# Attention with a learned position bias and two gated layers: an early table request on ScalarE and another order for the first two attention units

## The chip, the cores and the metric

The kernel runs on one core of one Trainium2 chip. The metric is the device time of an execution in microseconds (us); of several executions the median is given.

## The reference

Three stages follow one another, all in fp32. Only the first is touched by the change.

```python
# B, H, S, D = 2, 8, 576, 64
scores = q @ k.T / sqrt(D)
x = log1p(|i - j|) / log1p(max(i, 1))            # per pair of positions
bias = relu(x * w1 + b1) @ w2                    # 32 hidden units -> 8 heads
attn = softmax(scores + bias)                    # sum + 1e-9
x = attn @ v                                     # (1152, 512)
x = (silu(x @ w_gate) * (x @ w_val)) @ w_out     # 1536 hidden
# then a top-1 routed layer: 8 experts, capacity 288, 1024 hidden, relu
```

## The kernel before

**The bias.** For every position i the bias is a row over j. The kernel makes it in 36 groups of 16 rows. A group is: four `tensor_scalar` maxima on VectorE (`bias_t4`, line 107, tile `bt`, eight buffers), a product with `w2` on TensorE (`bias_mm`, line 125: eight matmuls), two evacuations on ScalarE that scale, add the constant `ncst` and mirror the row (`bias_evac`, lines 143 and 150, tile `bo`, four buffers), and a store by SP's queue to DRAM (line 154). `load_bias` (lines 165 to 167) reads the rows back, skewed, as a tile `bias_sb` of one block of 128 positions and one pair of heads. `ncst` is computed once at the start from `b1` and `w2` (a product of one column, folded by VectorE at line 313).

**The lead.** Eleven groups (`LEAD`) are made ahead of the attention loop. Between them, SP's queue issues further loads of queries and keys: after the store of the first group a query load and a key load, after that of the eighth another key load and the first two `load_bias`. The first scores (`qk(0)`) are computed after the tenth group, and the maxima of the twelfth are made before the loop starts.

**The units.** A unit is one block of 128 positions, one pair of heads and one batch: 32 of these, and four at the end that hold the last 64 positions of both batches. Every engine works its own queue in order, and the order is written out by hand: in each pass u of the loop, the names of the list `ORDER` are gone through, and each name issues its instructions if there is work for it. For head j = 0 or 1 of the pair the names are:

- `S`: VectorE adds the bias to the scores and takes the row minimum (line 203, tile `e_sb`)
- `E`: ScalarE's exponential with its sum (line 211)
- `R`: VectorE's reciprocal of the sum (lines 220 and 221)
- `N`: GpSimd normalises `e_sb` in place (line 225)

For the unit before it:

- `T0`, `T1`, `T2`: TensorE transposes three of the nine 128-column blocks of both heads (line 237, tile `ps_t`, two buffers); `T1` takes the end of the first head and the beginning of the second
- `V0`, `V2`: ScalarE evacuates the first and the last of these (line 248); `V1`: VectorE the middle one (line 246)

For the unit before that, `AV` is the product with the values and `XH`, `XL` its evacuation. `Q` computes the scores of the next unit (line 186). For the bias groups, counted from 0: `B0` to `B3` are the four maxima of group u + 12, `M0` and `M1` the product of group u + 11 (in two parts if its row is longer than 512 columns; a single part is `M1`), `BE0` and `BE1` its evacuation, `BE1` one pass later. `J` is a job for a later stage, none of which exists before pass 29.

In pass 0 there is no earlier unit. What is left of `ORDER` is S0 S1 B0 E0 E1 R0 B1 R1 Q B2 N0 B3 N1 M1; in pass 1 it is T0 S0 T1 S1 V1 BE1 B0 E0 E1 R0 B1 R1 V0 T2 Q B2 N0 B3 V2 N1 M1.

**After attention** the two projections, the output projection and routing, and the experts follow.

Of the kernel before, what the change touches and what calls it, by code (L numbers as in the profile page):

```python
# [14 lines left out]
AF = mybir.ActivationFunctionType  # L15
# [7 lines left out]

ORDER = (
    "G0 T0 S0 T1 G1 S1 V1 J AV BE1 B0 E0 E1 R0 J B1 M0 R1 J BE0 XH V0 T2 "
    "Q B2 XL J N0 B3 V2 N1 M1"
).split()

TAIL = [
    "T0 S0 T1 S1 E0 E1 V0 V1 R0 R1 N0 N1 AV XH T2 G0 XL V2 J J J J".split(),
    "T0 V0 T1 V1 AV T2 V2 XH XL G1".split(),
# [2 lines left out]
LEAD = 11  # L36
# [5 lines left out]
def attention(tc, ident, shape, qd, kd, vd, wb, geo, xh, xl, late):  # L42
    nc = tc.nc
# [16 lines left out]
    with ExitStack() as ctx:  # L60
# [15 lines left out]
        nc.sync.dma_start(geo_sb[:, :cut], geo[:, :cut])  # L76
        nbp, dist_sb, nips = geo_sb[:, :NB], geo_sb[:, NB:NB + S], geo_sb[:, NB + S:]
        ncst = cst.tile([P, 1], F32, name="ncst")
        kst = cst.tile([P, B * NP, S], F32, name="kst")
        vn = cst.tile([P, NP, B, NT_, 2 * D], F32, name="vn")  # L80
        bias_d = dr.tile([(S + 1) * H * PITCH], F32, name="bias_d")
# [20 lines left out]
        def bias_t4(R, a=0, b=4):  # L102
            m = span(R)
            for t4 in range(a, b):
                r = R * 4 + t4
                t = wk.tile([P, S], F32, tag="bt", name="bt", bufs=8)
                nc.vector.tensor_scalar(t[:, :m], dist_sb[:, :m], nbp[:, r:r + 1], None, ALU.max)  # L107
                bt_t[R, t4] = t
# [3 lines left out]
        def cuts(R):  # L112
            m = span(R)
            return [(0, m)] if m <= 512 else [(0, m // 2), (m // 2, m)]

        def bias_mm(R, part, wide=None):
            if part >= len(cuts(R)):
                return
            m0, m1 = cuts(R)[part]
            if wide is None:  # L120
                ps = ps_m.tile([P, 512], F32, tag="m", name="ps_b")
            else:
                ps = wide[part]
            for t4 in range(4):
                nc.tensor.matmul(
                    ps[t4 * GW:(t4 + 1) * GW, :m1 - m0], wb2, bt_t[R, t4][:, m0:m1], start=True, stop=True
                )
            bp_t[R, part] = ps
# [45 lines left out]
        groups = [c * GPC + n for c in order for n in range(GPC) if c * GPC + n < NG]  # L174
        NU = len(units)
# [126 lines left out]
        with tc.manual_schedule():  # L302
            korder = [(b, p) for p in range(NP) for b in range(B)]
            load_k(*korder[0])
            nc.sync.dma_start(geo_sb[:, cut:], geo[:, cut:])
            qt0 = order[0] * B
            load_q(qt0)
            nc.vector.tensor_scalar(dist_sb[:, :GEO0], dist_sb[:, :GEO0], w1c, None, ALU.mult)
            nc.vector.tensor_scalar(nbp, nbp, b1c, -1.0, ALU.mult, ALU.mult)
            ps_c = ps_m.tile([P, 512], F32, tag="m", name="ps_c")  # L310
            for t4 in range(4):
                nc.tensor.matmul(ps_c[t4 * GW:(t4 + 1) * GW, 0:1], wb2, b1c, start=True, stop=True)
            nc.vector.tensor_scalar_mul(ncst, ps_c[:, 0:1], -1.0 / SCALE)

            for n in range(LEAD):
                R = groups[n]
                bias_t4(R)
                if n < GPC:
                    wide = ps_s.tile([P, 2, 512], F32, tag="S", name="ps_w")
                    wide = wide[:, 0], wide[:, 1]  # L320
                elif n == GPC + 1:
                    wide = [
                        pool.tile([P, 512], F32, tag=tag, name="ps_w2") for pool, tag in ((ps_m, "m"), (ps_v, "x"))
                    ]
                else:
                    wide = [ps_t.tile([P, 512], F32, tag="T", name="ps_w2") for _ in cuts(R)]
                for part in range(2):
                    bias_mm(R, part, wide)
                if n == 0:
                    nc.vector.reciprocal(nips, nips)  # L330
                    nc.vector.tensor_scalar(dist_sb[:, GEO0:], dist_sb[:, GEO0:], w1c, None, ALU.mult)
                for part in range(2):
                    bias_evac(R, part)
                if n == 0:
                    load_q(qt0 + 1)
                    load_k(*korder[1])
                if n == GPC - 1:
                    load_k(*korder[2])
                    load_bias(order[0], 0)
                    load_bias(order[0], 1)  # L340
                elif n == GPC + 1:
                    qk(0)
            bias_t4(groups[LEAD])
            for u in range(NU + 2):
                n = LEAD + u
                g = groups[n] if n < NG else None
                g1 = groups[n + 1] if n + 1 < NG else None
                gp = groups[n - 1] if LEAD <= n - 1 < NG else None
                qc = order[u // 8 + 1] * B if u // 8 < NF else None
                if u < NU:  # L350
                    c, p, b = units[u]
                    for x in range(3, NU):
                        if units[x][2] in (0, None) and u == max(x - 2, x // 8 * 8 - 1, 0):
                            load_bias(*units[x][:2])
                    if u + 3 < len(korder):
                        load_k(*korder[u + 3])
                    if u % 2 == 0 and u // 2 < NP:
                        load_v(u // 2)
                    if RAW0 <= u < RAW0 + 4:
                        early_raw(*divmod(u - RAW0, 2))  # L360
                    if u % 4 == 0 and qc is not None:
                        load_q(qc + u % 8 // 4)
                live, prev, old = u < NU, 1 <= u <= NU, u >= 2
                two = g is not None and len(cuts(g)) == 2
                steps = {
                    "T0": (prev, lambda: transposes(u - 1, 0)),
                    "T1": (prev, lambda: transposes(u - 1, 1)),
                    "T2": (prev, lambda: transposes(u - 1, 2)),
                    "V0": (prev, lambda: t_evac(u - 1, 0)),
                    "V1": (prev, lambda: t_evac(u - 1, 1)),  # L370
                    "V2": (prev, lambda: t_evac(u - 1, 2)),
                    "BE1": (gp is not None, lambda: bias_evac(gp, len(cuts(gp)) - 1)),
                    "S0": (live, lambda: softmax(u, 0)),
                    "S1": (live, lambda: softmax(u, 1)),
                    "E0": (live, lambda: exp(u, 0)),
                    "E1": (live, lambda: exp(u, 1)),
                    "R0": (live, lambda: recip(u, 0)),
                    "R1": (live, lambda: recip(u, 1)),
                    "N0": (live, lambda: normalise(u, 0)),
                    "N1": (live, lambda: normalise(u, 1)),  # L380
                    "B0": (g1 is not None, lambda: bias_t4(g1, 0, 1)),
                    "B1": (g1 is not None, lambda: bias_t4(g1, 1, 2)),
                    "B2": (g1 is not None, lambda: bias_t4(g1, 2, 3)),
                    "B3": (g1 is not None, lambda: bias_t4(g1, 3, 4)),
                    "M0": (two, lambda: bias_mm(g, 0)),
                    "BE0": (two, lambda: bias_evac(g, 0)),
                    "M1": (g is not None, lambda: bias_mm(g, len(cuts(g)) - 1)),
                    "AV": (old, lambda: av(u - 2)),
                    "Q": (u + 1 < NU, lambda: qk(u + 1)),
                    "XH": (old, lambda: evac(u - 2, 0)),  # L390
                    "XL": (old, lambda: evac(u - 2, 1)),
                }
                for name in ORDER if u < NU - 1 else TAIL[u - NU + 1]:
                    if name == "J":
                        if u >= JOB0 and spare:
                            spare.pop(0)()
                    elif name in ("G0", "G1"):
                        if u == NU - 1 + int(name[1]):
                            gate0(int(name[1]))
                    elif steps[name][0]:  # L400
                        steps[name][1]()
                if u == NU:
                    late["idle"]()
                if u == NU - 1:
                    nc.scalar.activation(ncst, ncst, AF.Sigmoid)
                if u == NU + 1:
                    late["act"]((psg[0], psg[1]), wk.tile([P, S], F32, tag="bt", name="sg0", bufs=8))
# [824 lines left out]
```

## Time and profile before

| | |
|---|---|
| three timed executions | 591.12, 591.99, 592.31 us |
| their median | 591.99 us |
| the profiled execution | 588.43 us |
| its span, first to last instruction | 586.6 us |
| TensorE busy in the span | 535.1 us (91%) |
| VectorE busy | 393.5 us (67%) |
| ScalarE busy | 267.0 us (46%) |
| GpSimd busy | 93.3 us (16%) |
| mean granted TensorE clock | 0.961 of 2.4 GHz |

Rows of the trace are from the profiled execution, and times in them are us from the start of its span. PE is TensorE, PEld its weight load, DVE is VectorE, ACT is ScalarE, POOL is GpSimd, SPq is SyncE's queue. Ends of matmuls are modelled.

### The profile page before, as it was taken

The numbers are of one execution on the slowest core, as the hardware profiler recorded it, in microseconds if no ns is written. First come the engines' busy times: TensorE is split into PE (matmuls) and PEld (weight loads), VectorE is DVE, ScalarE is ACT, GpSimd is POOL, SyncE is SP. The second block draws the span as 40 slices with busy tenths as digits, with TensorE's granted clock in tenths as the row PEclk, the third lists the DMA queues.
The fourth block names the chain that finished last, engine by engine and source line by source line (L and its number), as shares of the span: only waits on it lengthen the run. The fifth ranks groups of instructions, "written<-read, shape, count | busy, mean of one in ns | idle before, by whom it ended". The sixth has DMA issues, their size and how long they took to land. (4 is left out here: it accounts for less than half of the span.)

```text
span 586.6 us, 10919 instructions
## 1 busy us (share of the span) xinstructions
PE 535.1 (91%) x3864; PEld 424.7 (72%) x3864; DVE 393.5 (67%) x1033; ACT 267.0 (46%) x578; POOL 93.3 (16%) x156
## 2 busy tenths in 40 slices
PE   6799999999999999999999999999979488299894
PEld 2366666666778899989999899997766285187673
DVE  7799999997776599999988475344451352244631
ACT  5677787787666345555343043222221150243420
POOL 0133333333333000000000000000231101210402
PEclk9899999999999999999999999999989879589898
DMA  5897436635331999854312121006119626900101
GB/s 189 293 318 236 142 122 198 197 113 183 110 84 57 286 357 341 297 184 160 108 73 94 50 80 65 1 31 258 46 61 340 234 83 254 322 4 1 44 1 44
DMA packets 49811, 88.87 MB, mean 151 GB/s; under 512 B 7986, under 2 KB 27444, under 8 KB 49728
## 3 DMA queue, kind: packets, MB, share of 16 engines
q1 hardware_dynamic: 48032, 84.11, 42.9%
q0 software_dynamic: 1552, 3.70, 1.8%
q8 instruction: 44, 0.72, 0.5%
q14 instruction: 39, 0.32, 0.2%
q10 hardware_dynamic: 144, 0.02, 0.0%
HBM read 66.73 MB, written 22.28 MB: 152 GB/s over the span
## 5 line engine op out<-in xcount | busy, mean ns | idle before, releaser
L488 PE MATMUL ps_gv<-xh,hl 128*128 128x384 f32 x528 | 135.5, 337 | 1.4 <-ACT hl L471 0.8
L488 PEld LDWEIGHTS ps_gv<-xh,hl 128*128 128x128 f32 x528 | 95.3, 188 | 2.8 <-ACT hl L471 1.5
L488 PE MATMUL ps_gv<-xl,hl 128*128 128x384 f32 x264 | 88.7, 336 | 0.0
L225 POOL TENSOR_SCALAR e_sb<-e_sb,rs 128x576 f32<-128x576 f32 x72 | 58.4, 821 | 127.4 <-DVE rs L221 98.4
L735 PE MATMUL ps_o<-hl,hh 128*128 128x512 f32 x216 | 72.4, 403 | 0.0
L107 DVE TENSOR_SCALAR bt<-geo_sb 128x320 f32<-128x320 f32 (+17 forms) x144 | 69.3, 517 | 0.0
L211 ACT ACTIVATE e_sb<-e_sb,mn 128x576 f32<-128x576 f32 x72 | 55.1, 768 | 15.9 <-DVE mn L203 15.9
L203 DVE CUSTOM_DVE_ANT_0 e_sb<-ps_s,bias_sb 128x576 f32<-128x576 f32 x72 | 51.3, 748 | 13.1 <-PE ps_s L186 5.9
L237 PEld LDWEIGHTS ps_t<-ident,e_sb 128*128 128x128 f32 x324 | 34.6, 142 | 30.8 <-POOL e_sb L225 15.3
L237 PE MATMUL ps_t<-ident,e_sb 128*128 128x128 f32 x324 | 52.0, 288 | 1.5 <-DVE et L246 1.1
L186 PE MATMUL ps_s<-kst,qst 64*128 64x288 f32 x320 | 49.3, 426 | 3.4 <-DVE mn L203 3.4
L488 PEld LDWEIGHTS ps_gv<-xl,hl 128*128 128x128 f32 x264 | 49.6, 188 | 0.1
L735 PEld LDWEIGHTS ps_o<-hl,hh 128*128 128x128 f32 x216 | 40.6, 188 | 10.0 <-issue 1.4
L559 POOL DMA_INDIRECT disp<-y,rsi x9 | 9.0, 1000 | 225.0 <-DVE rs L683 209.8
L735 PE MATMUL ps_o<-hl,hlo 128*128 128x512 f32 x105 | 42.1, 401 | 0.0
L266 PE MATMUL ps_x<-et,vn 128*64 128x128 f32 (+1 forms) x640 | 40.5, 269 | 0.0
L186 PEld LDWEIGHTS ps_s<-kst,qst 64*128 64x128 f32 x320 | 28.2, 186 | 15.3 <-issue 5.2
L471 ACT CAST hl<-dg 128x512 fp32r<-128x512 f32 x34 | 20.4, 620 | 39.0 <-PE ps_o L735 21.6
L498 ACT CAST hh<-sg 128x384 fp32r<-128x384 f32 x36 | 18.4, 511 | 38.3 <-DVE sg L497 38.0
L266 PEld LDWEIGHTS ps_x<-et,vn 128*64 128x64 f32 x640 | 31.7, 136 | 4.4
L248 ACT COPY et<-ps_t 128x384 f32<-128x384 f32 x72 | 31.2, 483 | 1.0 <-PE ps_t L237 1.0
L1059 PE MATMUL ps_h<-dxh,hl 128*128 128x288 f32 x128 | 29.5, 324 | 0.8 <-ACT dxh L458 0.8
(204 smaller groups left out, 910.1 us busy)
## 6 DMA issues: line engine op xcount, KB each, us to landing
raw<-e SPq DMA_DIRECT2D x24, 512.0 KB, 7.8
bias_d<-bo SPq DMA_DIRECT2D x36, 295.5 KB, 2.3
eraw<-e SPq DMA_DIRECT2D x16, 512.0 KB, 7.8
raw<-wo SPq DMA_DIRECT2D x12, 512.0 KB, 5.0
raw<-wg SPq DMA_DIRECT2D x11, 512.0 KB, 4.7
raw<-wv SPq DMA_DIRECT2D x11, 512.0 KB, 6.0
disp<-zero SPq DMA_DIRECT2D x9, 520.0 KB, 7.9
bias_sb<-bias_d SPq DMA_DIRECT2D x16, 288.0 KB, 3.6
```

The costliest lines, as they stand in the source:

```text
L107: nc.vector.tensor_scalar(t[:, :m], dist_sb[:, :m], nbp[:, r:r + 1], None, ALU.max)
L186: nc.tensor.matmul(pss[j][:, half, :HS], qst[c * B + bb][d, p], kst[d, bb * NP + p, half * HS:(half + 1) * HS], start=bb == bbs[0], stop=b ...
L203: nc.vector.tensor_tensor_reduce(out=e[:, j, :].rearrange("p (a n) -> p a n", a=2), in0=ps[:, :, :HS], in1=bias_sb[c, p][:, j, :].rearrang ...
L211: nc.scalar.activation(e[:, j, :], e[:, j, :], AF.Exp, bias=mn[:, j:j + 1], scale=-1.0, accum_out=sm[:, j:j + 1])
L225: nc.gpsimd.tensor_scalar(e[:, j, :], e[:, j, :], rs, 1.0, ALU.mult, ALU.mult)
L237: nc.tensor.transpose(ps[:, n * P:(n + 1) * P], e[:, o:o + P], ident)
L248: nc.scalar.copy(dst, ps)
L266: nc.tensor.matmul(ps[j * D:(j + 1) * D, o:o + n], vn[:, p, bb, jc, j * D:(j + 1) * D], et[:, t0:t0 + n], start=False, stop=jc == NF - 1, ...
L471: lambda: nc.scalar.copy(dh, g),
L488: nc.tensor.matmul(ps[:, :TN], w_[:, n, kc, :], x_[:, kc, t * TN:(t + 1) * TN], start=i == 0, stop=i == 3 * KC - 1,)
L735: nc.tensor.matmul(ps, ht_cols(f, a, tg), wot[f][b_], start=i == 0, stop=i == len(ops) - 1)
L1059: nc.tensor.matmul(ps[:, :CAP], part(e, f // 2, a)[:, kc, f % 2 * P:(f % 2 + 1) * P], x_[:, kc], start=i == 0, stop=i == 3 * KC - 1,)
```

## The change

At the start, ScalarE gets an exponential of one column, of a zero that VectorE has written to `ncst`. It stands behind the issue of the load of `wb_sb`, which is on ScalarE's queue too. `ncst` gets its value afterwards, as before.

Pass 0 and pass 1 have lists of their own. In pass 0 both reciprocals and both normalisations stand ahead of the four maxima, the scores of the next unit stand last (on TensorE, where they are alone now), and the product `M1` is gone. In pass 1 this product, of group 11, stands behind `T1` under the name `MF`. The rest of pass 1 is as before, `BE1` ahead of `E0` and `E1` too.

```diff
+FIRST = (
+    "S0 S1 E0 E1 BE1 R0 R1 N0 N1 B0 B1 B2 B3 Q"
+).split()
+SECOND = [x for step in ORDER for x in ((step, "MF") if step == "T1" else (step,))]
...
         ncst = cst.tile([P, 1], F32, name="ncst")
+        nc.vector.memset(ncst, 0.0)
+        nc.scalar.activation(ncst, ncst, AF.Exp)
...
             bias_t4(groups[LEAD])
+            assert len(cuts(groups[LEAD])) == 1
...
                     "M1": (g is not None, lambda: bias_mm(g, len(cuts(g)) - 1)),
+                    "MF": (True, lambda: bias_mm(gp, 0)),
...
-                for name in ORDER if u < NU - 1 else TAIL[u - NU + 1]:
+                for name in FIRST if u == 0 else SECOND if u == 1 else ORDER if u < NU - 1 else TAIL[u - NU + 1]:
```

## Rows read from the trace of the kernel before

**Rows 1.** Windows, from attention unit 2 on: busy time by engine, granted clock, DMA
```profile
core 0: us, PE busy (x) PEld busy (x) DVE busy (x) ACT busy (x) POOL busy (x), PEclk, DMA share, GB/s
30.00:120.00 90.00, 90.00 (x866) 56.90 (x865) 86.90 (x262) 68.48 (x169) 32.84 (x40) 1.00 0.61 199
```

**Rows 2.** Timeline of ScalarE, lead: start, duration, instruction, idle time before it
```profile
6.12 1.28 ACT L143 ACT_TABLE_LOAD   x1 [6.12 <-DVE geo_sb L330]
7.42 0.62 ACT L143 ACTIVATE bo<-ps_w,ncst,geo_sb 128x320 f32<-128x320 f32 x1
...
8.65 0.60 ACT L143 ACTIVATE bo<-ps_w,ncst,geo_sb 128x304 f32<-128x304 f32 x1
...
13.80 0.55 ACT L143 ACTIVATE bo<-ps_w,ncst,geo_sb 128x240 f32<-128x240 f32 x1 [0.93 <-PE ps_w L125]
```

**Rows 3.** Timeline of TensorE, lead: the last matmuls of the first and second group
```profile
5.76 1.33 PE L125 MATMUL ps_w<-bt,wb_sb 128*32 128x320 f32 x4
...
7.32 1.29 PE L125 MATMUL ps_w<-bt,wb_sb 128*32 128x304 f32 x4
```

**Rows 4.** Timeline of SP's queue, lead
```profile
8.53 0.33 SPq L154 DMA_DIRECT2D bias_d<-bo  x1
...
9.38 0.46 SPq L85 DMA_DIRECT2D kst<-kd  x1
9.95 0.36 SPq L154 DMA_DIRECT2D bias_d<-bo  x1
```

**Rows 5.** The tile `bo` from 9.9 to 10.0 us: the second store, issue to landing
```profile
DMA to landing us min/median/max: 3.7/3.7/3.7
```

**Rows 6.** Timeline of VectorE, late lead to unit 2
```profile
13.66 1.44 DVE L107 TENSOR_SCALAR bt<-geo_sb 128x384 f32<-128x384 f32 x4
...
22.82 0.76 DVE L203 CUSTOM_DVE_ANT_0 e_sb<-ps_s,bias_sb 128x576 f32<-128x576 f32 x1 [2.49 <-DMA bias_sb<-bias_d]
...
25.58 0.15 DVE L220 TENSOR_SCALAR rs<-sm 128x1 f32<-128x1 f32 x1
...
25.85 1.37 DVE L107 TENSOR_SCALAR bt<-geo_sb 128x384 f32<-128x384 f32 x2
27.13 0.74 DVE L203 CUSTOM_DVE_ANT_0 e_sb<-ps_s,bias_sb 128x576 f32<-128x576 f32 x1
...
28.94 0.56 DVE L246 COPY et<-ps_t 128x384 f32<-128x384 f32 x1 [0.38 <-PE ps_t L237]
...
30.30 0.15 DVE L220 TENSOR_SCALAR rs<-sm 128x1 f32<-128x1 f32 x1
...
31.93 0.74 DVE L203 CUSTOM_DVE_ANT_0 e_sb<-ps_s,bias_sb 128x576 f32<-128x576 f32 x1
```

**Rows 7.** Timeline of TensorE, units 0 to 2
```profile
23.64 0.75 PE L186 MATMUL ps_s<-kst,qst 64*128 64x288 f32 x2 [3.06 <-DVE mn L203]
...
25.87 1.56 PE L125 MATMUL ps_b<-bt,wb_sb 128*32 128x400 f32 x8
27.36 1.54 PE L237 MATMUL ps_t<-ident,e_sb 128*128 128x128 f32 x6
29.55 0.55 PE L237 MATMUL ps_t<-ident,e_sb 128*128 128x128 f32 x3 [0.65 <-DVE et L246]
...
34.04 0.55 PE L237 MATMUL ps_t<-ident,e_sb 128*128 128x128 f32 x3
...
35.69 0.83 PE L125 MATMUL ps_b<-bt,wb_sb 128*32 128x368 f32 x8
```

**Rows 8.** Timeline of ScalarE, units 0 and 1
```profile
27.55 0.69 ACT L143 ACTIVATE bo<-ps_b,ncst,geo_sb 128x400 f32<-128x400 f32 x1 [2.00 <-issue]
...
28.53 0.77 ACT L211 ACTIVATE e_sb<-e_sb,mn 128x576 f32<-128x576 f32 x1
...
29.95 0.19 ACT L211 ACTIVATION_READ_ACCUMULATOR e_sb<-e_sb,mn 128x1 f32 x1
```

**Rows 9.** Timeline of GpSimd, unit 0
```profile
25.43 1.57 POOL L225 TENSOR_SCALAR e_sb<-e_sb,rs 128x576 f32<-128x576 f32 x2 [24.13 <-DVE rs L221]
```

**Rows 10.** Windows, unit 0 to 1 (columns as in rows 1)
```profile
25.80:29.20 3.40, 3.10 (x15) 1.34 (x14) 3.02 (x8) 1.65 (x4) 1.20 (x2) 0.50 1.05 328
```

## The prediction

> **What bounds the kernel now.** I read the busy time by stage first, then the queues of the first 35 us one engine at a time, because the change touches nothing later. The stage view [rows 1] shows TensorE busy for the whole of 30 to 120 us and VectorE for 86.9 of these 90: from attention unit 2 on, TensorE is the bound, with VectorE close behind. Time that is won or lost before about 34 us is therefore a shift of TensorE's start into that stretch, and it is carried to the end; the 586.6 us span lies in an execution of 588.43 us, 3.56 us below the median of the three timed runs (591.99), so I work out a difference on the profile and lay it on the median.
>
> In the lead (4 to 23 us) the first evacuation by ScalarE starts at 7.42 us, right behind a table load of 1.28 us [rows 2]. The reader should not take 1.28 us for the price. The first group's product ends at 5.76 + 1.33 = 7.09, so without the load the evacuation would wait until then; the second group's product ends at 7.32 + 1.29 = 8.61, and the second evacuation starts at 8.65, so that one was not held by the load at all [rows 2, 3].
>
> What can carry the first 0.33 us further is SP's queue. The first store of bias rows (8.53) stands ahead of a query load and a key load (9.38), and the second store (9.95) takes 3.7 us to land, because it travels behind them [rows 4, 5]. The sixth evacuation waits at 13.80 [rows 2] for that landing, as there are four `bo` buffers. From there copy, product, store and re-load lead to the first softmax, which waits at 22.82 for `bias_sb` [rows 6].
>
> In units 0 and 1 the order is: TensorE does the bias product M1 of unit 0 at 25.87, then the transposes T0 and T1 of unit 0 at 27.36, then idles until T2 at 29.55, which waits for the evacuation V1 [rows 7]. ScalarE evacuates M1 (BE1) at 27.55 and starts the first exponential of unit 1 at 28.53, as soon as BE1 lets it [rows 8].
>
> **The change part by part.**
>
> *The table load.* It moves to ScalarE's empty start. Its new writer and reader of `ncst` cost VectorE one memset and one wait before the fold of the constant; both lie before 4.5 us beside the first loads, when ScalarE has nothing else to do: nothing, at most some 0.1 us if the wait became an instruction of its own. The gain is 7.42 − 7.09 = 0.33 us for the first evacuation and the first store. The two loads and the second store move with it, and through the sixth evacuation the first softmax too. Bounds: 0 if the landing of the second store is not the last to come at 13.80, 0.33 by the products' ends, 1.28 if these ends are modelled far too late. I take **−0.3 us**.
>
> *FIRST on VectorE and GpSimd.* The reciprocals R0 and R1 go ahead of the four maxima of the thirteenth group. R0 comes some 0.3 us earlier, so GpSimd's first normalisation does too. R1 does not: it starts at 25.58 now, when the second exponential's sum arrives. So N1, the second normalisation, still ends at 25.43 + 1.57 = 27.00 [rows 6, 9]. Two of the maxima that filled VectorE's wait now follow R1: with 1.44 us for four they are 0.36 us each, 0.7 us together [rows 6]. Unit 1's first softmax goes from 27.13 to about 27.8. Price by itself +0.3 us at V1: it starts now at 28.94 after 0.38 us of idle time, and the idle time goes.
>
> The skill speaks to this: the Trainium skill, "SBUF — State Buffer", section "SBUF: two separate sides", says that VectorE in its two-port mode and GpSimd hold one port pair in turn, each for a whole instruction. The row agrees in that two maxima take 1.37 us beside the normalisations against 0.36 us each alone; by the rule a third could be caught, which would make the 0.7 us about 1.0.
>
> *M1 of unit 0 becomes MF behind T1.* Its eight matmuls are the same. TensorE can start T0 at about 25.9, 1.4 us earlier. But T1 covers the end of head 0 and the beginning of head 1, so it needs N1: it starts at about 27.05. Six transposes take 1.54 us in this stretch, three 0.7 [rows 7]. So MF starts at about 27.75. From M1's start to BE1 the present distance is 27.55 − 25.87 = 1.68 us; BE1 starts at 29.4 instead of 27.55, and behind it in ScalarE's in-order queue stand both exponentials of unit 1. BE1 takes 28.53 − 27.55 = 0.98, so the first exponential goes from 28.53 to 30.4, **1.85 us** later, though its softmax is ready by about 28.6.
>
> What waits for it: R0 and R1 of unit 1. R1 starts at 30.30 now, with its sum there at 29.95 + 0.19 = 30.14 [rows 6, 8], so 0.15 us is slack: R1 goes to 30.30 + 1.85 − 0.15 = 32.0, VectorE idles for it, and the first softmax of unit 2 goes from 31.93 to 33.6. Behind it come V1 and then T2 of unit 1 on TensorE, 34.04 now [rows 7]; T2 there has some 0.1 us to give, as it stands behind TensorE's own products too. **+1.6 us** for TensorE. The first transposes' lead of 1.4 us buys nothing against this, since V1 waits for VectorE and V0 for ScalarE.
>
> This is with the products at half clock: granted 0.50 from 25.80 to 29.20 [rows 7, 10], which is 1.2 of 2.4 GHz, after TensorE had idled 3.06 us up to 23.64. At full clock a bias product takes 0.83 us where this one takes 1.56, and three transposes 0.55 [rows 7]. Then T1 ends at about 27.5, BE1 starts at about 28.45, the first exponential at 29.4 and R1 at 30.30 + 0.87 − 0.15 = 31.0. Unit 1 of the kernel before would be faster as well, by VectorE's idle time before V1, with R1 at 30.30 − 0.38 = 29.9. The loss is 1.1 us, or **+1.0 us** for TensorE.
>
> The Trainium skill, "TensorE: Matmul & The Clock Gate", section "What's actually happening", says that the clock's checks run freely and don't start with the kernel, so that the number of slow matmuls differs from run to run. By it the timed runs would be a mixture of both cases. No row here shows a second execution.
>
> **Sum.** Half clock −0.3 + 1.6 = +1.3; full clock −0.3 + 1.0 = +0.7. I take the middle, +1.0: 591.99 + 1.0 = **593.0 us**, own range 592.4 to 593.7. The least that this kernel's timing can tell from no change is 0.2%, 1.18 us.
>
> **The rivals.**
>
> *Paid back or hidden (0 to −0.3 us, 591.7 to 592.0).* TensorE's share of 30 to 40 us is from modelled ends; if VectorE or a load sets the pace and leaves gaps, the late start is taken up within the 36 units, or in the weight loads that follow attention. For it: VectorE and TensorE are nearly equally full. Against it: TensorE's row is full to the last hundredth over 90 us.
>
> *Faster: the head gains everything.* If the first product is really done by 6.1, the first store is 1.28 us earlier and the second lands before 13.0. For it: ends of matmuls are modelled. Against: the second evacuation starts 0.04 us after such an end [rows 2, 3]. It decides only if the exponentials lose less than 0.1 us; with the 0.38 us of VectorE idle time won as well the sum is −1.66: 590.3.
>
> *The load in the way.* ScalarE also issues the load of `wb_sb`, which VectorE's first instruction waits for. If the table load ran ahead of that issue, all would start 1.28 us later: +1.28 − 0.3 + 1.0 = 2.0, 594.0. Against it: the issue has no wait and stands first.
>
> **Chances.** The forecast's own mechanism 0.65, paid back 0.2, faster 0.08, load in the way 0.07. The forecast straddles 1.18 us, as its half-clock end lies above: I give 0.3 of its 0.65 to slower and 0.35 to same. Together slower 0.3 + 0.07 = 0.37; same 0.35 + 0.2 = 0.55 less 0.03 for chance in where the clock falls later, which I give to faster: 0.52 and 0.11. Range 591.4 to 594.0: from the paid-back case's lower end with 0.3 us for the scatter of the three runs to the load in the way; what lies outside is the faster case and the far tails.
>
> **What the profile after would show.** The table load before 3 us and the first evacuation at about 7.1; the first softmax at about 22.5 (−0.3). T0 at about 25.6, T1 at 26.8, the product right behind. ScalarE idle from about 25.3 to 28 or 29, then BE1, and only then unit 1's first exponential, with VectorE idle before R0 and R1 of unit 1; T2 of unit 1 at 34.8 to 35.4 instead of 34.04; from there the same spacing. Wrong would be: an exponential of unit 1 that starts before 28.6, T2 of unit 1 at or before 34.0 (then the time falls), or a distance to the kernel before that shrinks between 40 and 190 us.

## The result and the profile after

The changed kernel takes 595.81 us (median of 12 runs, 593.42 to 598.11) against 592.15 us for the kernel before (median of 12 runs): ratio 1.0058, interval 1.004 to 1.0076, or 3.7 us slower. The forecast was 593.0 us, range 591.4 to 594.0. The time lies outside that range.

Line numbers of the changed kernel are those of the kernel before plus 7 in attention's functions and plus 9 in the later stages. I read its start first, engine by engine.

ScalarE's timeline of the changed kernel, lead and units 0 and 1 (answers to [rows 2, 8]):

```profile
1.16 1.28 ACT L85 ACT_TABLE_LOAD   x1 [1.16 <-PEq L1231]
2.45 0.20 ACT L85 ACTIVATE ncst<-ncst 128x1 f32<-128x1 f32 x1
7.21 0.62 ACT L150 ACTIVATE bo<-ps_w,ncst,geo_sb 128x320 f32<-128x320 f32 x1 [4.56 <-PE ps_w L132]
...
30.04 0.68 ACT L150 ACTIVATE bo<-ps_b,ncst,geo_sb 128x400 f32<-128x400 f32 x1 [4.60 <-issue]
30.62 0.50 ACT L157 ACTIVATE bo<-ps_b,ncst,geo_sb 128x191 f32<-128x191 f32 x1
31.02 0.77 ACT L218 ACTIVATE e_sb<-e_sb,mn 128x576 f32<-128x576 f32 x1
```

The table load sits in the empty start, and the first evacuation comes 0.21 us earlier than in [rows 2]. Then ScalarE idles for 4.6 us ahead of BE1, and unit 1's first exponential waits behind BE1: 31.02 instead of 28.53 [rows 8].

VectorE's timeline, units 0 to 2 (answers to [rows 6]):

```profile
22.86 0.76 DVE L210 CUSTOM_DVE_ANT_0 e_sb<-ps_s,bias_sb 128x576 f32<-128x576 f32 x1 [2.43 <-DMA bias_sb<-bias_d]
...
25.47 0.15 DVE L227 TENSOR_SCALAR rs<-sm 128x1 f32<-128x1 f32 x1 [0.56 <-ACT e_sb L218]
25.66 0.16 DVE L228 RECIPROCAL rs<-rs 128x1 f32<-128x1 f32 x1
25.74 1.80 DVE L114 TENSOR_SCALAR bt<-geo_sb 128x384 f32<-128x384 f32 x4
27.46 0.75 DVE L210 CUSTOM_DVE_ANT_0 e_sb<-ps_s,bias_sb 128x576 f32<-128x576 f32 x1
...
29.86 0.41 DVE L114 TENSOR_SCALAR bt<-geo_sb 128x368 f32<-128x368 f32 x1 [0.50 <-PE ps_b L132]
31.91 0.15 DVE L227 TENSOR_SCALAR rs<-sm 128x1 f32<-128x1 f32 x1 [1.64 <-ACT e_sb L218]
...
34.11 0.74 DVE L210 CUSTOM_DVE_ANT_0 e_sb<-ps_s,bias_sb 128x576 f32<-128x576 f32 x1
```

The first softmax is where it was (22.86, before 22.82): some 0.2 us of the lead's gain are still there when the re-load is issued (19.08, before 19.28), and they are lost by the time it lands. The 1.64 us of idle time at 31.91 is VectorE waiting for the late exponential, and unit 2's first softmax comes at 34.11 instead of 31.93. The 0.50 us at 29.86 is a wait that the prediction did not have: the next maximum needs the buffer that the late product still reads.

TensorE's timeline, units 0 to 2 (answers to [rows 7]), and the windows of the same stretch and of [rows 1]:

```profile
23.68 3.20 PE L193 MATMUL ps_s<-kst,qst 64*128 64x288 f32 x8 [3.02 <-DVE mn L210]
26.81 1.54 PE L244 MATMUL ps_t<-ident,e_sb 128*128 128x128 f32 x6
28.28 1.56 PE L132 MATMUL ps_b<-bt,wb_sb 128*32 128x400 f32 x8
29.77 0.90 PE L244 MATMUL ps_t<-ident,e_sb 128*128 128x128 f32 x3
...
36.06 0.55 PE L244 MATMUL ps_t<-ident,e_sb 128*128 128x128 f32 x3 [0.34 <-DVE et L253]
```

```profile
core 0: us, PE busy (x) PEld busy (x) DVE busy (x) ACT busy (x) POOL busy (x), PEclk, DMA share, GB/s
24.00:30.40 6.40, 6.40 (x25) 3.23 (x24) 5.12 (x16) 1.75 (x5) 1.75 (x2) 0.50 1.02 352
30.00:120.00 90.00, 88.91 (x851) 56.17 (x851) 85.34 (x259) 69.62 (x170) 31.04 (x38) 1.00 0.62 195
```

T2 of unit 1 is at 36.06 instead of 34.04, and TensorE has 1.1 us of idle time in the window from 30 us that was full before [rows 1]. The clock is at half (0.50, 1.2 of 2.4 GHz) from 23.7 us, where the engine had idled 3.02 us, not from 25.8 as in [rows 10]. From 36 us to the end of attention the distance stays at 2.0 us; at 434 us, after the output projection, it is 2.2 us. So attention accounts for some 2 us between these two profiles, and the rest arises in the experts; the two profiled executions lie 8.4 us apart in span, more than the medians do.

There the idle time ahead of TensorE's transposes of the next expert's rows (tile `ps_x`) changes. TensorE's weight loads, the first two such transposes, in the changed kernel and in the kernel before:

```profile
458.96 0.72 PEld L889 LDWEIGHTS ps_x<-ident,xd 128*128 128x128 f32 x4 [5.15 <-issue]
...
477.37 0.72 PEld L889 LDWEIGHTS ps_x<-ident,xd 128*128 128x128 f32 x4 [7.37 <-issue]
```

```profile
452.63 0.42 PEld L880 LDWEIGHTS ps_x<-ident,xd 128*128 128x128 f32 x4 [1.05 <-issue]
...
470.50 0.72 PEld L880 LDWEIGHTS ps_x<-ident,xd 128*128 128x128 f32 x4 [8.93 <-issue]
```

The first waits 4.1 us longer, the second 1.6 us less: 2.5 us more in sum. "issue" says that no semaphore held the engine. What held it were branches, jumps that are decided while the kernel runs (the experts' code is chosen by the number of rows): the trace has 42 branches on TensorE, with 37.5 us in sum after and 32.1 us before. The page's list of DMA queues shows one thing more, a fetch of instructions (q8), in the changed kernel and in the kernel before:

```profile
q8 instruction: 45, 0.74, 0.5%
```

```profile
q8 instruction: 44, 0.72, 0.5%
```

45 packets instead of 44, each of 0.74 MB / 45 = 16.4 kB. The long branches wait for such packets: each of the 124 branches over 1.7 us in the twenty traces here has a packet of this queue that ends inside it, and the branch ends 1.32 to 1.74 us after the last such end; of the 716 short ones 56 overlap a packet at all. TensorE's stream, all the instructions of its queue in their order, has one instruction more than before: the matmuls are the same 3864, but the product MF needs one wait as an instruction of its own (121 of these instead of 120).

### The profile page after: what moved, and what is told of

Its sections match the earlier page's. It is cut to its first block, busy times and chain, and to the rows that moved or that the text cites. A ratio compares the mean times of both kernels' runs of the same rounds, so it can differ in the third digit from the quotient of the medians.

```text
span 595.0 us, 10923 instructions
## 1 busy us (share of the span) xinstructions
PE 539.6 (91%) x3864; PEld 425.8 (72%) x3864; DVE 393.5 (66%) x1034; ACT 266.8 (45%) x579; POOL 95.3 (16%) x156
## 5 line engine op out<-in xcount | busy, mean ns | idle before, releaser
L193 PE MATMUL ps_s<-kst,qst 64*128 64x288 f32 x320 | 50.5, 433 | 3.0 <-DVE mn L210 3.0
L255 ACT COPY et<-ps_t 128x384 f32<-128x384 f32 x72 | 31.1, 481 | 1.1 <-PE ps_t L244 1.1
```

Of the source, the lines that this page charges most:

```text
L193: nc.tensor.matmul(pss[j][:, half, :HS], qst[c * B + bb][d, p], kst[d, bb * NP + p, half * HS:(half + 1) * HS], start=bb == bbs[0], stop=b ...
L255: nc.scalar.copy(dst, ps)
```

## The experiments

Three theories. A: unit 1's exponentials stand behind BE1, which waits for MF. B: VectorE's order FIRST costs. C: the experts' branches cost more because TensorE's stream is one instruction longer, whatever the change does in attention. The rival to C is that the extra time in the experts follows from the late start of attention.

This table holds what all the runs gave. Length is the number of instructions in TensorE's stream ahead of the experts' branches, against the kernel before. q8 is the number of instruction fetches of that queue in the profile. Branches is the sum over TensorE's 42 branches in the trace (us); the one "at 450 us" of the expectations is the one that ends the first expert. T2 is T2 of unit 1 (us). Half clock is the stretch of the start with TensorE's clock granted at 1.2 GHz (us). Ratios are to the kernel before on the same chip in the same session.

| kernel | length | q8 | branches | T2 | half clock | ratio, interval |
|---|---|---|---|---|---|---|
| before | 0 | 44 | 32.1 | 34.04 | 25.8 to 29.2 | 1 |
| changed | +1 | 45 | 37.5 | 36.06 | 23.7 to 30.5 | 1.0058, 1.004 to 1.0076 |
| table_only | 0 | 44 | 33.2 | 35.43 | 24.0 to 30.8 | 1.0007, 0.9985 to 1.0029 |
| order_only | +1 | 45 | 36.4 | 35.58 | 25.7 to 29.1 | 1.0055, 1.0034 to 1.0075 |
| copy_behind_exp | +1 | 45 | 36.4 | 33.95 | 25.4 to 28.8 | 1.0049, 1.0028 to 1.007 |
| mf_alone | +1 | 45 | 36.1 | 36.28 | 24.2 to 31.0 | 1.006, 1.0038 to 1.0083 |
| first_keeps_m1 | 0 | 44 | 34.0 | 34.13 | 25.3 to 28.7 | 0.9988, 0.9975 to 1.0002 |
| before_pad | +4 | 44 | 32.1 | 35.16 | 23.0 to 29.8 | 1.0, 0.998 to 1.002 |
| after_len | −3 | 44 | 34.4 | 36.27 | 22.7 to 29.5 | 1.0018, 1.0 to 1.0036 |
| behind_exp_len | −3 | 44 | 35.1 | 34.37 | 25.4 to 28.8 | 0.9997, 0.9981 to 1.0013 |
| before_p1 | +1 | 45 | 36.1 | 35.21 | 23.5 to 30.3 | 1.007, 1.0044 to 1.0095 |
| before_len | −4 | 44 | 34.0 | 34.96 | 22.7 to 29.5 | 1.0015, 0.9993 to 1.0037 |
| after_zero | 0 | 44 | 32.2 | 36.15 | 24.5 to 31.3 | 1.0009, 0.9993 to 1.0024 |
| behind_exp_zero | 0 | 44 | 32.7 | 34.17 | 25.7 to 29.2 | 0.9997, 0.998 to 1.0014 |
| before_m8 | −8 | 44 | 34.4 | 34.84 | 22.5 to 29.3 | 1.0024, 1.0004 to 1.0044 |
| before_p32 | +32 | 43 | 31.1 | 37.70 | 25.2 to 35.4 | 0.9969, 0.9949 to 0.9989 |
| before_p48 | +48 | 43 | 31.0 | 37.30 | 24.6 to 34.9 | 0.9937, 0.9912 to 0.9962 |
| before_warm | +48 | 43 | 30.4 | 34.98 | none | 0.9933, 0.9911 to 0.9956 |
| after_warm | +49 | 43 | 30.8 | 34.94 | none | 0.9942, 0.9925 to 0.996 |
| copy_warm | +49 | 43 | 31.2 | 34.19 | none | 0.9927, 0.9902 to 0.9952 |

**The parts of the change.** The early request alone, in the kernel before:

```diff
+        nc.vector.memset(ncst, 0.0)
+        nc.scalar.activation(ncst, ncst, AF.Exp)
```

> The early table request alone, both lists as before. Theory A (the loss is ScalarE's: unit 1's exponentials stand behind a copy of MF's product) expects the second transposes' evacuation and T2 of unit 1 within 0.3 us of 34.04 and a time within 0.5 us of the kernel before. Rival B (VectorE's order in pass 0 is the loss) expects the same. Rival C (part of the loss lies in the experts' branches, and it follows the length of TensorE's instruction stream, one longer in the changed kernel) expects the same as well, since this stream has the old length. A time 1.5 us or more above before would speak for the early request itself.

Measured: ratio 1.0007, no difference. Its T2 is late (35.43, not within 0.3 us of 34.04 as expected), though attention's order is that of before: the clock was at half from 24.0 us, and the first softmax came at 23.47. By itself the request neither gains nor costs anything that these runs can tell (−0.9 to 1.7 us).

The changed kernel without these two lines:

> Both lists of the change, without the early table request. A: T2 of unit 1 at about 36.1 (+2.0 us), carried to the end of attention; time +2 us. C: the same and 1 to 2 us more in the experts, +3 to +4 us in all. B: +2 us too, so this run does not part A from B.

Measured: ratio 1.0055, as the whole change. Here the clock fell where it fell in the profile of before, so that this profile can be laid on [rows 6 to 8] step by step:

```profile
27.84 1.50 PE L130 MATMUL ps_b<-bt,wb_sb 128*32 128x400 f32 x8
...
35.58 0.55 PE L242 MATMUL ps_t<-ident,e_sb 128*128 128x128 f32 x3 [0.34 <-DVE et L251]
```

```profile
29.55 0.68 ACT L148 ACTIVATE bo<-ps_b,ncst,geo_sb 128x400 f32<-128x400 f32 x1 [3.78 <-issue]
...
30.52 0.77 ACT L216 ACTIVATE e_sb<-e_sb,mn 128x576 f32<-128x576 f32 x1
```

The product at 27.84, BE1 at 29.55, the exponential at 30.52 and T2 of unit 1 1.54 us late lie near the prediction's half-clock case (27.75, 29.4, 30.4, 1.6). Part of that is chance: the first softmax of this execution came 0.34 us later than in [rows 6] (23.16), which no part of the change explains, and from there T2 is 1.20 us late.

The changed kernel with BE1 behind unit 1's second exponential in pass 1:

```diff
-SECOND = [x for step in ORDER for x in ((step, "MF") if step == "T1" else (step,))]
+SECOND = [x for step in ORDER if step != "BE1" for x in {"T1": ("T1", "MF"), "E1": ("E1", "BE1")}.get(step, (step,))]
```

> The changed kernel with BE1 moved behind E1 in pass 1, nothing else. A: unit 1's first exponential at about 28.3 instead of 31.02, T2 of unit 1 at 34.5 or earlier, so at most 0.5 us of the lag of 2.0 is left; time within 0.6 us of before if there is nothing but A, and 1 to 2 us above it if C holds, as TensorE's stream is the longer one here. B: a lag of 1.5 us or more is left, since VectorE's order is untouched.

Measured: attention loses nothing any more. ScalarE's and TensorE's timelines of this kernel:

```profile
28.30 0.78 ACT L218 ACTIVATE e_sb<-e_sb,mn 128x576 f32<-128x576 f32 x1 [2.89 <-DVE mn L210]
...
29.83 0.67 ACT L150 ACTIVATE bo<-ps_b,ncst,geo_sb 128x400 f32<-128x400 f32 x1
```

```profile
33.95 0.55 PE L244 MATMUL ps_t<-ident,e_sb 128*128 128x128 f32 x3
```

The exponential now waits for its softmax, T2 of unit 1 is 0.1 us earlier than in [rows 7] (0.2 us later when both are taken from the first softmax, which came at 22.53): A makes attention's loss. Yet the kernel is 2.9 us slower than before (0.0049 × 592), with the branches at 36.4 us. A is not what costs most of the time.

The early request, the old order in pass 0 without M1, and MF behind T1:

```diff
-FIRST = (
-    "S0 S1 E0 E1 BE1 R0 R1 N0 N1 B0 B1 B2 B3 Q"
-).split()
+FIRST = ORDER[:-1]
```

> The early request and MF behind T1, but pass 0 in the old order without M1. A: unit 1's first exponential later than 30, T2 of unit 1 at +1.5 to +2.0 us, time +1.5 to +2 us (and 1 to 2 more by C). B: T2 within 0.4 us of 34.04, time within 0.6 us of before.

Measured: 1.006, T2 at 36.28: the late product alone makes the whole loss, in both stages. And the reverse, the new order FIRST with M1 kept at its end and the old order in pass 1:

```diff
-    "S0 S1 E0 E1 BE1 R0 R1 N0 N1 B0 B1 B2 B3 Q"
+    "S0 S1 E0 E1 BE1 R0 R1 N0 N1 B0 B1 B2 B3 Q M1"
...
-SECOND = [x for step in ORDER for x in ((step, "MF") if step == "T1" else (step,))]
+SECOND = ORDER
```

> The early request and the new order FIRST of unit 0, but with the bias product M1 at the end of unit 0 and the old order in unit 1: TensorE's stream has before's length. The theory that ScalarE's copy behind the late product makes attention's loss expects T2 of unit 1 within 0.5 us of 34.04 or, with the half clock's earlier start, up to 35.4 as in table_only; the stream's length expects a branches' sum of 32 to 34 us. Time 591.5 to 592.8. If it is the order FIRST on VectorE that costs: T2 of unit 1 at 36 and 594 or more.

Measured: 0.9988 and T2 at 34.13, 0.1 us from before. B falls.

**The length of TensorE's stream.** One idle product of one column in the lead of the kernel before, four instructions:

```diff
+            ps_n = ps_v.tile([P, 512], F32, tag="x", name="ps_n")
+            nc.tensor.matmul(ps_n[:GW, 0:1], wb2, b1c, start=True, stop=True)
```

> The kernel before with one idle product of one column, in fp32, added to the end of TensorE's lead: four more instructions in TensorE's stream from there on, and nothing else. The theory that the experts' stage loses time because TensorE's stream is of another length there (branches that wait for code, 36 to 37.5 us in all against 32 to 33) expects those branches to change with no cause in attention: the last attention product within 0.3 us of before, the branches' sum off by 2 us or more from 32.1, and the time off by as much, either way (590 or 594 us). The theory that the extra time in the experts' stage follows from the late start of attention expects 591.5 to 592.3 and a sum of 32 to 33.

Measured: 1.0. The branch at 450 us went from 0.48 to 4.99 us, as C says, but the one at 460 us from 4.19 to 1.72 and one at 470 us from 2.84 to 0.20: the sum stayed at 32.1. So the length moves the waits between branches, but the expectation that the sum would change was wrong for this length. The clock was at half from 23.0 us here, with attention's order of before:

```profile
core 0: us, PE busy (x) PEld busy (x) DVE busy (x) ACT busy (x) POOL busy (x), PEclk, DMA share, GB/s
23.20:29.60 6.40, 5.88 (x21) 2.88 (x22) 5.05 (x16) 2.57 (x6) 1.56 (x2) 0.50 1.02 349
```

Its T2 is at 35.16, 1.1 us behind [rows 7]. The profile of the kernel before thus shows the kinder of two cases that its own order has.

The changed kernel, and copy_behind_exp, with one idle product less of the twelve that stand ahead of the experts (three empty instructions, `nop`, are written beside it; the trace has no record of them, and its count is three below before's):

```diff
-    WARM = 12
+    WARM = 11
```

> The changed kernel with one idle product less of the twelve ahead of the experts (a product that computes nothing that is used), which takes four instructions out of TensorE's stream ahead of the experts' branches: one more than before becomes three less. If the stream's length sets what the branches cost, their sum leaves 37.5 us, by 2 us or more, and the time leaves 595.8; at a sum as before's it is 594.0, with the 2.0 us that attention loses. If the extra time follows from the late start in attention, the time stays at 595.5 to 596 and the sum at 37.

> The changed kernel with the copy BE1 behind unit 1's second exponential (as in copy_behind_exp, whose attention lost nothing) and with one idle product less ahead of the experts, as in after_len. By the stream's length: T2 of unit 1 at 34.0 as in copy_behind_exp, branches' sum as in after_len's, and a time that is 2.0 us below after_len's: 591.5 to 592 if the sum is as before's. If the experts' extra time has another cause in the changed order: 594, as copy_behind_exp.

Measured: 1.0018 and 0.9997, with 44 fetches each. Four instructions less give back 0.004 × 592 = 2.4 us of the changed kernel and 3.1 us of copy_behind_exp (0.0052 × 592). In the profiled executions the sums are 34.4 and 35.1 us; the profiled execution of behind_exp_len was among its slowest.

The kernel before with exactly one instruction more: an idle product that needs one wait (four and one) in the lead, and one product less of the twelve (four):

```diff
+            pa = cst.tile([P, GW], F32, name="pa")
+            pb = cst.tile([P, 1], F32, name="pb")
+            nc.gpsimd.memset(pa, 0.0)
+            nc.vector.memset(pb, 0.0)
+            ps_n = ps_v.tile([P, 512], F32, tag="x", name="ps_n")
+            nc.tensor.matmul(ps_n[:GW, 0:1], pa, pb, start=True, stop=True)
...
-    WARM = 12
+    WARM = 11
```

> The kernel before with exactly one instruction more in TensorE's stream from the experts on: one idle fp32 product of one column in the lead (four instructions and one wait) and one idle product of the twelve ahead of the experts taken out (four). Attention and its order are before's. By the stream's length: the branch at 450 us waits 5 to 6 us as in the four kernels with one more, the branches' sum is 36 to 37.5, and the time 2 to 3 us over before, ratio 1.0035 to 1.005. By any cause in the changed order (a late attention, another fill of the queues): branch 0.5 us, sum 32 to 33, ratio 0.998 to 1.002.

Measured: 1.007 with a sum of 36.1 us, a ratio somewhat above the expected one, with no line of attention's order changed. Weight loads of `ps_x` in this kernel:

```profile
457.72 0.71 PEld L886 LDWEIGHTS ps_x<-ident,xd 128*128 128x128 f32 x4 [4.94 <-issue]
...
476.28 0.71 PEld L886 LDWEIGHTS ps_x<-ident,xd 128*128 128x128 f32 x4 [7.02 <-issue]
```

These are the waits of the changed kernel, 5.15 and 7.37. The control without the idle product in the lead (only `WARM = 11`):

> The kernel before with one idle product of the twelve ahead of the experts taken out, nothing else: the control for the kernels that use this to set the length. Length minus four: the branch at 450 us waits 4 to 5 us, those at 460 to 475 us less than before's, sum 32 to 35, time 590.5 to 592.5 (ratio 0.997 to 1.001), as the kernels of length minus three and plus four. If the product taken out saves time by itself (0.2 us of TensorE): not more than 0.2 us of this.

Measured: 1.0015, no clear difference, sum 34.0 us; the branch at 450 us took 3.1 us, less than the 4 to 5 expected. The other direction, the changed kernel and copy_behind_exp brought back to before's length by an idle transpose (two and one wait) and `WARM = 11`:

```diff
+            pb = cst.tile([P, 1], F32, name="pb")
+            nc.vector.memset(pb, 0.0)
+            ps_n = ps_v.tile([P, 512], F32, tag="x", name="ps_n")
+            nc.tensor.transpose(ps_n[:1, :P], pb, ident)
...
-    WARM = 12
+    WARM = 11
```

> The changed kernel with TensorE's stream brought back to before's length at the experts: one idle transpose in the lead (two instructions and one wait), one idle product of the twelve ahead of the experts taken out (four). By the stream's length: T2 of unit 1 at 36 (attention still loses 2.0 us), the branch at 450 us at 0.5 us, sum 32 to 34, time 2.0 us over before: ratio 1.0025 to 1.0045. If the experts' loss follows from the late attention or from the changed order: branch 5 to 6 us, sum 36 to 37.5, ratio 1.005 to 1.0075.

> The changed kernel with BE1 behind unit 1's second exponential and with TensorE's stream at before's length, as in after_zero: both causes taken away. T2 of unit 1 at 34.0, branch at 450 us 0.5 us, sum 32 to 34, ratio 0.998 to 1.001. If a third cause is left: ratio above 1.002.

Measured: 1.0009 and 0.9997. Weight loads of `ps_x` in after_zero:

```profile
454.58 0.42 PEld L893 LDWEIGHTS ps_x<-ident,xd 128*128 128x128 f32 x4 [1.05 <-issue]
...
473.39 0.72 PEld L893 LDWEIGHTS ps_x<-ident,xd 128*128 128x128 f32 x4 [9.31 <-issue]
```

The waits are close to those of before again (1.05, 8.93), while T2 of unit 1 is as late as in the changed kernel (36.15). C is shown in both directions: one instruction added to the kernel before makes the loss, and the changed kernel at the old length has lost all but 0.5 us of it (interval −0.4 to 1.4). I had expected 1.0025 to 1.0045 here, with attention's 2.0 us kept; the time shows less than the profiles' T2 (M1 as MF, below, comes back to this). The rival falls: attention's late start is there, and the experts do not lose.

**Other lengths, and the clock.** The kernel before with two idle products less of the twelve (`WARM = 10`), and with eight idle products of one column in the lead (before_pad's, eight times):

> The kernel before with two idle products of the twelve ahead of the experts taken out: length minus eight. If before's length is one of a few lucky ones: branch at 450 us 3 to 6 us, branches' sum 34 to 37.5, time 591 to 596. If a loss is the exception: sum 32 to 34, time as before.

> The kernel before with eight idle products of one column in the lead: length plus 32. As before_m8: a lucky length of before gives 3 to 6 us at the branch at 450 us and a sum of 34 to 37.5, the other view 32 to 34. The eight products may make the first bias product up to 1 us late, and with it attention.

Measured: 1.0024 with 44 fetches, and 0.9969 with 43, although the eight products brought T2 to 37.70. The first came out as for a lucky length of before (sum 34.4, time up by 0.2 to 2.6 us; only the branch at 450 us, 2.7, stayed just under 3), the second as neither view had it (branch 5.9, sum 31.1). So before's length is better than some and not the best. Twelve idle products in TensorE's wait ahead of the first attention product, in the kernel before and in the changed one:

```diff
             bias_t4(groups[LEAD])
+            warm = ps_v.tile([P, 512], F32, tag="x", name="ps_warm0")
+            for _ in range(12):
+                nc.tensor.matmul(warm[:, :P], ident, ident, start=True, stop=True)
```

> The kernel before with 12 idle products in TensorE's wait ahead of the first attention product (20.6 to 23.6 us), 48 instructions. If they keep the clock at full through 24 to 31 us: no half clock in that stretch, T2 of unit 1 at 33.3 to 33.8, where before has 34.0 (half for 3.4 us) or 35.0 to 35.2 (half for 6.8 us), and attention gains 0.5 us on the one and 1.5 us on the other. If the clock falls all the same: 34.0 to 35.2. The branches' sum at length plus 48 is not known: 32 to 38.

> The changed kernel with the same 12 idle products (length plus 49). At full clock the prediction's step gives +1.0 us for T2 of unit 1 against before_warm's: 34.3 to 34.8; if the late copy costs 2 us whatever the clock: 35.3 to 35.8. If FIRST and MF cost nothing at full clock: within 0.2 us of before_warm's. Branches' sum within 1 us of before_warm's unless one instruction matters at this length too.

Measured: 0.9933 and 0.9942, both faster than before. In before_warm the clock stays up, and the second of the two waits goes from 8.93 to 2.10 us (windows, then weight loads of `ps_x`):

```profile
24.20:30.60 6.40, 4.43 (x28) 2.38 (x30) 6.13 (x22) 4.79 (x12) 1.70 (x3) 1.00 0.98 326
```

```profile
457.08 0.72 PEld L883 LDWEIGHTS ps_x<-ident,xd 128*128 128x128 f32 x4 [4.29 <-issue]
...
469.19 0.42 PEld L883 LDWEIGHTS ps_x<-ident,xd 128*128 128x128 f32 x4 [2.10 <-issue]
```

T2 came later than I expected from a full clock (34.98, not 33.3 to 33.8): VectorE now sets the pace of units 0 and 1 (TensorE waits 1.53 us for V1), the first softmax was 0.8 us later in this execution (23.66), and the value product waited 0.46 us for a load. And after_warm's T2, at 34.94, is level with it, which by my expectation says that FIRST and MF cost nothing at full clock:

```profile
34.98 0.55 PE L237 MATMUL ps_t<-ident,e_sb 128*128 128x128 f32 x3
```

```profile
34.94 0.55 PE L244 MATMUL ps_t<-ident,e_sb 128*128 128x128 f32 x3 [0.33 <-DVE et L253]
```

From the first softmax, which came at 23.27 in after_warm, its T2 is 0.35 us later than before_warm's, and without the wait for the load in before_warm it would be some 0.8 us (an estimate: 0.35 + 0.46). One more instruction at this length changed neither the fetches nor the time. before_warm holds two edits in one, a longer stream and a higher clock. The same length with almost no work (products of one column and 32 rows at the same place):

```diff
+                nc.tensor.matmul(warm[:GW, 0:1], wb2, b1c, start=True, stop=True)
```

> As before_warm, with idle products of one column and 32 rows in place of its 128 by 128: the same 48 instructions at the same place, little work. If the gain of before_warm (3.9 us) is the stream's length: half clock for 3.4 to 6.8 us in the start as in before, T2 of unit 1 at 34.0 to 35.2, the branches as in before_warm (5 us at 451 us, 0.2 to 0.3 at those of 465 and 469), sum 30 to 31.5, ratio 0.993 to 0.997. If it is the clock: ratio 0.998 to 1.001.

Measured: 0.9937 with T2 at 37.30, over 2 us later than in before_warm and later than I expected, as the clock stayed at half for 10.2 us in this profile. The gain is the length's, not the clock's. Where all of it lies isn't shown: from the first branch to the end the profile takes 141.6 us against 144.2 before, and the branches' sum accounts for 1.1 us of these 2.6. What the clock adds at this length (before_warm against before_p48) lies within the intervals. Last, the changed kernel with BE1 behind the second exponential and the twelve idle products:

> The changed kernel with BE1 behind unit 1's second exponential and the 12 idle products of after_warm (length plus 49, as there). The first exponential of unit 1 comes 1.0 to 1.7 us sooner than in after_warm, measured from the first softmax; if attention's loss is from that copy, T2 of unit 1 comes 0.3 to 1.0 us sooner by the same measure, and the ratio is 0.992 to 0.994. If the late copy costs nothing at full clock: as after_warm within 0.2 us.

Measured: 0.9927, the lowest ratio, not distinguishable from before_warm's. Its exponential starts 1.35 us sooner than in after_warm (28.54 against 29.89) and T2 0.75 us sooner; from the first softmax it is 1.24 and 0.64 us. That is what the late copy costs at full clock.

## Why the prediction was wrong

**The step that failed** is the first: "the change touches nothing later", and with it that the shift in the start is all that reaches the end. The shift itself was carried (2.0 us at unit 1, 2.2 us at 429 us in the profiles). But the change also touched the length of TensorE's stream, and with it which of the experts' branches wait for a fetch of instructions. Between after_zero and the changed kernel lie 0.0049 × 592 = 2.9 us, between behind_exp_zero and copy_behind_exp 0.0052 × 592 = 3.1 us, and one instruction alone cost 4.1 us (interval 2.6 to 5.6). No rival had a loss outside the start. Forecast 1.0 plus 2.9 is 3.9 us; measured are 3.7.

The number of fetches orders all the kernels: 45 fetches give ratios of 1.0049 to 1.007, 44 of 0.9988 to 1.0024, 43 of 0.9927 to 0.9969; the branches' sums fall in the same order (36.1 to 37.5, 32.1 to 35.1, 30.4 to 31.2 us). The Trainium skill, "Runtime: NRT & Kernel Launch", section "Instruction fetch mechanics", says that instructions are streamed in blocks of 16 KiB, read ahead in sequence only, and that a taken branch to a block that isn't there stalls until it is fetched. This case's traces agree: packets of 16.4 kB, and of the 840 branches of the twenty profiles 716 take 0.06 to 0.68 us and 124 take 1.72 to 7.67 us, none a time between; a packet ends inside each of the 124. That one added instruction moves a jump's target across a block's edge fits both, but no run shows which instruction lies in which block. It stays open why, of the lengths tried, the branch at 450 us is short only at before's.

**The table load**: the mechanism stood as far as the re-load: the first evacuation at 7.21 (forecast 7.1), the sixth at 13.53 instead of 13.80, where it waits for the store's landing as the prediction said, and the re-load's first issue 0.20 us sooner. Its size at the first softmax was 0 in the mean, not −0.3. In the eleven kernels with the early request whose profiles I have, that softmax lies between 22.22 and 23.47 us, mean 22.94; in the six without it and with the lead otherwise little changed (before, order_only, before_pad, before_p1, before_len, before_m8) between 22.80 and 23.16, mean 22.94. So the head's gain is not seen behind the re-load's landing; with this scatter a few tenths of a us either way can't be told. The rival with the load in the way did not occur: the load starts at 1.16, behind the issue at 0.73.

**FIRST**: right in kind, forecast too large. Unit 1's first softmax came 0.33 us later, not 0.7 (27.46, forecast 27.8). By itself, in first_keeps_m1, FIRST put V1 off by 0.1 us instead of 0.3 (29.03 against 28.94) and T2 by 0.1 us.

**M1 as MF**: right in mechanism, its size somewhat too large. At a like clock T2 is late by 1.54 us, or 1.20 from the first softmax, against 1.6 (order_only). At full clock it is 0 as the profiles lie, 0.35 from the first softmax (after_warm against before_warm), and 0.64 to 0.75 for the copy's place alone (after_warm against copy_warm), against 1.0. In the profile after, all steps came some 0.4 to 0.6 us later than forecast, since the clock fell 2.1 us earlier and the scores took 3.20 us. Where the half clock starts between 22 and 25 us and lasts for 6.8 us, five profiles without MF show T2 at 34.84 to 35.43 (before_pad, before_p1, before_len, before_m8, table_only; mean 35.12), four with it at 36.06 to 36.28 (changed, mf_alone, after_len, after_zero; mean 36.19): 1.07 us apart. So the 2.0 us between the two profiles are some 1 us of change and 1 us of clock, by these means. The times say the same: four pairs that differ in the place of BE1 alone (changed and copy_behind_exp, after_len and behind_exp_len, after_zero and behind_exp_zero, after_warm and copy_warm) lie 0.0009, 0.0021, 0.0012 and 0.0015 apart, 0.5 to 1.2 us, each within its noise and all the same way. The clock fell at anything from 22.5 to 25.8 us in kernels whose start is nearly the same. That agrees with the Trainium skill, "TensorE: Matmul & The Clock Gate", section "What's actually happening", by which the clock's checks run freely and do not start with the kernel. Of the seventeen profiles with a stretch at half clock nine have 6.8 us of it, two 10.2 us, and six, that of before among them, 3.4 us.

**The sum**: without the extra fetch the forecast's +1.0 us lies within the interval of after_zero (−0.4 to 1.4 us), whose middle is 0.5. Part of this is luck: the sum took off 0.3 us for the head, which brought nothing, and put 1.3 us on for M1, where about 1 is seen. The rival "paid back" is not excluded by that interval, but TensorE's distance did not shrink in attention (2.02 us at unit 1, 2.01 at the last value product).

## What to carry over

Where a kernel branches at run time, a change's price can have a term that has nothing to do with its place: compare the number of instruction fetches and the waits named "issue" behind the branches, not only the stage that was edited. When a small change moves the time by more than its stage can explain, add and take away idle instructions at the old order; here this told 3 us from 1 in two runs, and a longer stream gave 0.6% with next to no work. And one profile of either kernel is one draw: the spans of the two profiles differ by 8.4 us, the medians by 3.7.

## What the hardware showed

- At before's length, a stream longer by one instruction costs 2.9 to 4.1 us of 592; 48 more, almost without work, save 3.7 us (0.0063 × 592), and with a 49th fetches and time stay as they are (43 and 0.9942 in after_warm, 43 and 0.9933 in before_warm).
- A branch on TensorE takes 0.06 to 0.68 us or 1.72 to 7.67 us, and each long one ends 1.32 to 1.74 us after a packet of the instruction queue has ended.
- The same order in attention ran with TensorE's clock at half from 25.8 to 29.2 us in one profile and from 23.0 to 29.8 us in another. Twelve idle products in the wait ahead of it kept the clock at 1.00.
- ScalarE's first instruction behind the table load started as the load ended (1.16 + 1.28 = 2.44, start 2.45).
